# ScalarE before VectorE at the bank of transposed queries, and one ring of three PSUM banks in place of two and one

## The chip, the core and the metric

The kernel runs on one core of a Trainium2 chip. Five engines with queues of their own work side by side: TensorE (matmuls and transposes, written to PSUM as banks of 128 rows x 512 fp32), VectorE (DVE), ScalarE (ACT), GpSimd (POOL) and SyncE (SP, which issues most DMAs). They meet at semaphores. The metric is the device time of one execution in microseconds.

## What is computed

Causal attention with a gated memory part (4 batches, 8 heads, 576 rows, head size 64), and behind it a mixture of four experts with fixed weights per row, all in fp32:

```python
scores = scale * q @ k.T                       # causal, softmax -> a
local = a @ v
q_p = where(q > 0, q, exp(q) - 1) + 1
mem_out = (q_p @ M_prev) / (q_p @ z_prev + 1e-6)
x = g * mem_out + (1 - g) * local              # g = sigmoid(beta)
for e in range(4):
    out += p[:, e] * (relu(x @ w1[e]) @ w2[e])  # x: 2304 x 512, w1: 512 x 1024
```

## The kernel before

The expert part runs on TensorE with operands split in a high and a low fp32r half, three products for each. Its work comes in phases (one expert and half of its hidden columns for the row groups then open); mm1 makes the hidden tile h, ScalarE writes hh (L885) and VectorE hl (L886), mm2 makes y, and VectorE adds it to acc (L923). w_prep (L212) splits the weights: a cast on ScalarE (L225) or GpSimd (L227), then the difference on GpSimd (L228). The last eight of 24 phases handle the remaining rows in another form and hold no attention.

Attention of two heads of one batch is a task. The first run is written out by hand (first_run); 28 more tasks are cut into steps, and steps and parts of expert phases are issued alternately by a planner (the loop at the end), so that TensorE has matmuls of the expert part between the small pieces of attention. The first 12 tasks (query chunks 0 and 1, up to 188 us) are of the joint kind, the last 16 (chunks 2 to 4; their t_trq between 195 and 602 us) of the second kind. The order on every engine is the order of issue.

A task transposes queries (t_trq, tile tq), keys (t_trk, tk) and phi(q) (t_trqp, tp); s_qk makes scores (sp), VectorE masks them, ScalarE takes the exponential and scales; s_pt transposes the probabilities (tile pt, L353), evicted by ScalarE to pth (L660) and by VectorE to ptl (L662); s_o makes the output tile o, evicted by otmp (L573) and xr (L584). GpSimd scales phi(q) in place (qp, L345).

PSUM's eight banks: two for scores (tag qk), three for the expert part (moe), two in a ring for tq, tk, tp, o and the small transposes of the fifth chunk (tag to, function to_tile), and one for pt. A new tile of a ring waits for the last reader of the tile that had its bank. Two engines that read the same bank are also put one after the other, in the order of issue.

In t_trq of the second kind the bank tq is read by twelve instructions: split_q (ScalarE qa, qb; VectorE qa, qb, the low halves), split_k for 64 key columns (ScalarE kha, khb; VectorE kl twice), then four ScalarE copies to qz (L403). As issued, each group waits for the one before it.

Of the kernel before, what the change touches and what calls it, by code (L numbers as in the profile page):

```python
# [8 lines left out]
F32 = mybir.dt.float32  # L9
# [4 lines left out]
PSUM = bass.MemoryType.PSUM  # L14
# [35 lines left out]
def tile_attention_moe(  # L50
# [14 lines left out]
    P = 128  # L65
    B, H, S, D = q.shape
    NT, DM = out.shape
    E, _, F = w1.shape
# [5 lines left out]
    SCALE = -1.0 / (D ** 0.5)  # L74
# [34 lines left out]
    sp = ctx.enter_context(tc.tile_pool(name="sp", bufs=2))  # L109
    ps = ctx.enter_context(tc.tile_pool(name="ps", bufs=1, space=PSUM))  # L110
    own = ExitStack()
    att = own.enter_context(tc.tile_pool(name="att", bufs=2))

    def ctile(shape, dt, name, pool=cst):
# [23 lines left out]
    for i in range(2):  # L138
        o, d = i * 13 * P, {}
# [213 lines left out]
        nc.tensor.transpose(dst, src, ident[0:n, 0:n])  # L353

    def to_tile(name):
        return ps.tile([P, 512], F32, tag="to", name=name, bufs=2)

    A, Bh = slice(0, D), slice(D, P)

    def split_q(pt, qa, qb, n, scale):  # L360
        nc.scalar.activation(qa[A, 0:n], pt[A, 0:n], AF.Copy, scale=scale)
        nc.scalar.activation(qb[Bh, 0:n], pt[Bh, 0:n], AF.Copy, scale=scale)
        nc.vector.scalar_tensor_tensor(
            qa[Bh, 0:n], pt[A, 0:n], scale, f(qa[A, 0:n]), ALU.mult, ALU.subtract
        )
        nc.vector.scalar_tensor_tensor(
            qb[A, 0:n], pt[Bh, 0:n], scale, f(qb[Bh, 0:n]), ALU.mult, ALU.subtract
        )

    def split_k(pt, qk, c0, n, joint=False):  # L370
        o = slice(c0, c0 + n)
        for x, k_ in ((A, qk["kha"]), (Bh, qk["khb"])):
            nc.scalar.activation(k_[x, o], pt[x, 0:n], AF.Copy)
        for h, (x, k_) in enumerate(((A, qk["kha"]), (Bh, qk["khb"]))):
            l_ = qk["qz"][x, h * GW : h * GW + n] if joint else qk["kl"][x, o]
            nc.vector.tensor_tensor(l_, pt[x, 0:n], f(k_[x, o]), ALU.subtract)
# [12 lines left out]
    def t_trq(t):  # L389
        pt = to_tile(f"tq{t.i}")  # L390
        qk, last = t.qk, t.nk == NCH
        w = len(t.cs) * P
        for i in range(len(t.cs)):

            tr(pt[:, i * P : (i + 1) * P], flat(t.nat["q"][:, i]), P)
        if last:
            tr(pt[:, w : w + P], flat(t.nat["k"][:, 4]), P)
        split_q(pt, qk["qa"], qk["qb"], w, SCALE)
        if last:
            split_k(pt[:, w:], qk, 4 * P, D)  # L400
            for h, x in enumerate((A, Bh)):
                for o, a, b_ in ((h * GW, 0, GW), (2 * GW + h * D, w - D, w)):
                    nc.scalar.activation(  # L403
                        qk["qz"][x, o : o + b_ - a], pt[x, a:b_], AF.Copy, scale=SCALE
                    )

    def t_cpq(t):
        dup_k(t.qk, 4 * P, D, copier(t))

    def t_trk(t):  # L410
        pt = to_tile(f"tk{t.i}")
        m = min(t.nk, NCH - 1)
        for c in range(m):
            tr(pt[:, c * P : (c + 1) * P], flat(t.nat["k"][:, c]), P)
        split_k(pt, t.qk, 0, m * P, t.joint)
        if t.joint:
            t_cpk(t)

# [107 lines left out]
    def j_pt(i):  # L526
        s = slots[i]
        c, t = s.c, s.t
        qc = slice(c * P, (c + 1) * P)
        pt = ps.tile([P, 512], F32, tag="pt", name=f"pt{i}", bufs=1)  # L530
        pt = pt[:, 0 : 2 * (c + 1) * P].rearrange("p (h j q) -> p h j q", h=2, q=P)
        for hd in range(2):
            for j in range(c + 1):
                tr(pt[:, hd, j], s.s3[:, hd, j * P : (j + 1) * P], P)
        s.p4 = {
            x: PT[t.i % 2][x].rearrange("p j q -> p (j q)")[:, 0 : 4 * GW].rearrange(
                "p (h j q) -> p h j q", h=2, q=GW
            )
            for x in "hl"
        }  # L540
        dh, dl = (s.p4[x][:, :, 0 : c + 1, qc] for x in "hl")
        if c == 0:
            pt, dh, dl = pt[:, :, 0], dh[:, :, 0], dl[:, :, 0]
        nc.scalar.activation(dh, pt, AF.Copy)
        nc.vector.tensor_tensor(dl, pt, f(dh), ALU.subtract)
# [118 lines left out]
    def s_pt(i, last=False):  # L664
        s = slots[i]
        c, t = s.c, s.t
        qo = c * P - t.q0
        if last:
            pt = to_tile(f"pt{i}_4")

            m = rows(4)
            tr(pt[0:m, 0:P], s.s[:, 4 * P : S], P)
            src = pt[0:m, 0:P].rearrange("p (h q) -> p h q", h=2)
            hi = [PT[h]["h"][:, 4, qo : qo + D] for h in range(2)]
            evict([(src[:, h], hi[h][0:m], hi[h][m:P]) for h in range(2)])
            return
        pt = ps.tile([P, 512], F32, tag="pt", name=f"pt{i}", bufs=1)
        n = min(c + 1, 4)
        for j in range(n):
            tr(pt[:, j * P : (j + 1) * P], s.s[:, j * P : (j + 1) * P], P)  # L680
        if c < 4:
            src = pt[:, 0 : n * P].rearrange("p (j q) -> p j q", q=P)
            evict([(src, *(PT[s.hd][x][:, 0:n, qo : qo + P] for x in "hl"))])
        else:
            src = pt.rearrange("p (j h q) -> p h j q", j=4, h=2)
            evict(
                [(src[:, h], *(PT[h][x][:, 0:n, qo : qo + D] for x in "hl")) for h in range(2)]
            )
# [95 lines left out]
    for i, s in slots.items():  # L784
        w = wid(s.c)
# [184 lines left out]

    def open_last():
        own.close()
        pool = fin["pool"] = ctx.enter_context(tc.tile_pool(name="fin", bufs=1))

        def new(shape, dt, name):
            return pool.tile(shape, dt, tag=name, name=name, bufs=1)

        fin["x"] = {
            n: [new([P, 2, DM], F32R, f"{n}{z}") for z in "hl"]
            for n in ("b11", "t1", "t2", "b21", "t3", "t4", "b22")  # L980
        }
        fin["w"] = [
            new([P, 2, 7, GW], F32R, "wu"),
            w1all[:, 0 : 14 * GW].rearrange("p (z n f) -> p z n f", z=2, n=7),
        ]
        fin["s"] = [new([P, 4, GW], F32, f"sw{j}") for j in range(1)]

    def x_steps():
        x = fin["x"]
        t_ = {}  # L990

        def raw(k, c):
            return xr[:, 2 * (k // 2) + c, DM * (k % 2) : DM * (k % 2) + DM]

        def hi(n, c, src):
            nc.scalar.activation(x[n][0][:, c], src(), AF.Copy)

        def lo(n, c, src, eng):
            eng.tensor_tensor(x[n][1][:, c], src(), f(x[n][0][:, c]), ALU.subtract)

        def diff(n, c, tag, a, b_):
            t_[n, c] = ps.tile([P, 512], F32, tag=tag, name=f"{n}_{c}", bufs=2)
            nc.vector.tensor_tensor(t_[n, c], a(), b_(), ALU.subtract)

        V, G = nc.vector, nc.gpsimd
        out_ = []

        def both(fn, *args):
            out_.extend(lambda c=c: fn(c, *args) for c in range(2))

        def get(k, c):
            return t_[k, c] if isinstance(k, str) else raw(k, c)

        def D_(c, n, tag, a, b_):
            diff(n, c, tag, lambda: get(a, c), lambda: get(b_, c))

        def H_(c, n, k):
            hi(n, c, lambda: get(k, c))

        def L_(c, n, k, eng):  # L1020
            lo(n, c, lambda: get(k, c), eng)

        both(H_, "b11", 0)
        both(D_, "t1", "qk", 1, 0)
        both(L_, "b11", 0, V)
        both(H_, "t1", "t1")
        both(D_, "t2", "to", 3, "t1")
        both(L_, "t1", "t1", V)
        both(H_, "t2", "t2")
        both(D_, "t4", "qk", 2, "t2")  # L1030
        both(L_, "t2", "t2", V)
        both(H_, "t4", "t4")
        both(D_, "t3", "to", 3, 1)
        both(L_, "t4", "t4", V)
        both(H_, "t3", "t3")
        both(L_, "t3", "t3", V)
        late = len(out_)
        both(H_, "b21", 2)
        both(L_, "b21", 2, G)
        both(H_, "b22", 3)  # L1040
        both(L_, "b22", 3, G)
        return out_[:late], out_[late:]
# [43 lines left out]
    def pass_parts(i):  # L1086
# [5 lines left out]
        def prod(pr, key, wn, xn, new):  # L1092
            def run():
                if new:
                    tag, nb = {"x": ("to", 2), "z": ("qk", 2), "y": ("pt", 1)}[key]
                    bank[pr, key] = ps.tile(
                        [P, 512], F32, tag=tag, name=f"{key}{i}_{pr}", bufs=nb
                    )
                k_, n = bank[pr, key], 0
# [130 lines left out]
    def first_run():  # L1230
# [110 lines left out]
        def f_pt(i):  # L1341
# [2 lines left out]
            ptp[i] = (  # L1344
                moe_bank(f"ptf{i}")
                if c
                else ps.tile([P, 512], F32, tag="pt", name=f"ptf{i}", bufs=1)
            )
            pt4 = ptp[i][:, 0 : 2 * (c + 1) * P].rearrange("p (h j q) -> p h j q", h=2, q=P)
            for hd in range(2):  # L1350
# [167 lines left out]
    with tc.manual_schedule():  # L1518
# [7 lines left out]
        for i in range(2):  # L1526
            nc.gpsimd.memset(f(QK[i]["qz"]), 0.0)
            nc.gpsimd.memset(f(QK[i]["qa"][:, 3 * P :]), 0.0)
        first_run()
        phases = [phase_parts(i) for i in range(PASS)]  # L1530
        pcost = [sum(c for c, _ in ph) for ph in phases]

# [88 lines left out]
```

## Time and profile before

| | us |
|---|---|
| median of three runs | 1000.37 (999.36 to 1000.77) |
| profiled execution | 1000.42 |
| its span | 998.6 |
| TensorE busy | 983.3 |
| VectorE / ScalarE / GpSimd busy | 650.7 / 565.9 / 593.3 |

TensorE is the engine that is never long idle. Its ends are modelled in the profile, so that the distance from one start to the next is the surer measure of a lost time. VectorE, ScalarE and GpSimd are idle a third of the span or more; their idle time matters only where TensorE waits for what they do next.

### The profile page before, as it was taken

The numbers are of one execution on the slowest core, as the hardware profiler recorded it, in microseconds if no ns is written. First come the engines' busy times: TensorE is split into PE (matmuls) and PEld (weight loads), VectorE is DVE, ScalarE is ACT, GpSimd is POOL, SyncE is SP. The second block draws the span as 40 slices with busy tenths as digits, with TensorE's granted clock in tenths as the row PEclk, the third lists the DMA queues.
The fourth block names the chain that finished last, engine by engine and source line by source line (L and its number), as shares of the span: only waits on it lengthen the run. The fifth ranks groups of instructions, "written<-read, shape, count | busy, mean of one in ns | idle before, by whom it ended". The sixth has DMA issues, their size and how long they took to land.

```text
span 998.6 us, 16042 instructions
## 1 busy us (share of the span) xinstructions
PE 983.3 (98%) x5118; PEld 824.7 (83%) x5118; DVE 650.7 (65%) x1668; ACT 565.9 (57%) x1350; POOL 593.3 (59%) x601
## 2 busy tenths in 40 slices
PE   8999999999999999999999999999999999999998
PEld 6889878877888888888888888888888888888887
DVE  6888887878877777777788787755244252442533
ACT  7687866666666677766666666554334243242430
POOL 6898856755754667756574655386363563635620
PEclk9999999999999999999999999999999999999999
DMA  6676544544443345554444433131121121111102
GB/s 166 177 196 170 142 129 122 151 118 118 127 112 100 94 139 161 149 138 115 109 126 118 106 90 87 43 127 55 51 64 43 48 59 53 54 42 53 53 1 85
DMA packets 185268, 102.16 MB, mean 102 GB/s; under 512 B 96224, under 2 KB 163552, under 8 KB 185184
## 3 DMA queue, kind: packets, MB, share of 16 engines
q1 hardware_dynamic: 184880, 101.00, 37.1%
q8 instruction: 41, 0.67, 0.3%
q14 instruction: 43, 0.35, 0.1%
q10 hardware_dynamic: 304, 0.14, 0.1%
HBM read 90.09 MB, written 4.72 MB: 95 GB/s over the span
## 4 chain that ended last, share of the span: by engine, by line
PE 82%; DVE 6%; ACT 4%; POOL 3%; issue 3%; DMA 2%; SPq 0%; POOLq 0%; ACTq 0%; DVEq 0%
PE h L876 18%; PE y L1184 17%; PE y L907 16%; PE x L1106 9%; PE z L1106 4%; PE pt L353 3%; PE o L721 3%; PE sp L611 3%; PE y L1106 2%; POOL w2l L228 1%; POOL w L228 1%; DMA stg<-in_moe_w_dram 1%; PE sp L473 1%; PE o L559 1%; DVE acc L923 1%
## 5 line engine op out<-in xcount | busy, mean ns | idle before, releaser
L228 POOL TENSOR_TENSOR w2l<-stg,w2h 128x512 fp32r<-128x512 f32 x128 | 168.0, 1316 | 152.4 <-ACT w2h L225 147.7
L876 PE MATMUL h<-xh,w 128*128 128x512 f32 (+1 forms) x768 | 246.8, 371 | 0.0
L228 POOL TENSOR_TENSOR w<-stg,w 128x512 fp32r<-128x512 f32 x96 | 127.1, 1329 | 153.5 <-ACT w L225 133.7
L876 PEld LDWEIGHTS h<-xh,w 128*128 128x128 f32 x768 | 139.3, 190 | 17.7 <-POOL w L228 0.4
L876 PE MATMUL h<-xl,w 128*128 128x512 f32 (+1 forms) x384 | 137.0, 357 | 0.0
L907 PE MATMUL y<-w2h,hh 128*128 128x512 f32 x320 | 135.8, 424 | 0.5 <-DVE hl L886 0.5
L907 PE MATMUL y<-w2l,hh 128*128 128x512 f32 x320 | 125.8, 393 | 1.0 <-POOL w2l L228 1.0
L907 PE MATMUL y<-w2h,hl 128*128 128x512 f32 x320 | 126.3, 395 | 0.0
L1201 DVE SCALAR_TENSOR_TENSOR acc<-y,pn,acc 128x512 f32<-128x512 f32 (+1 forms) x57 | 41.6, 740 | 82.2 <-PE y L1184 82.2
L876 PEld LDWEIGHTS h<-xl,w 128*128 128x128 f32 x384 | 73.2, 191 | 5.8
L660 ACT ACTIVATE pth<-pt 128x384 fp32r<-128x384 f32 (+3 forms) x128 | 49.6, 419 | 47.6 <-PE pt L353 46.7
L907 PEld LDWEIGHTS y<-w2h,hl 128*128 128x128 f32 x320 | 60.0, 188 | 14.3 <-DVE hl L886 0.8
L907 PEld LDWEIGHTS y<-w2l,hh 128*128 128x128 f32 x320 | 60.6, 189 | 10.1 <-POOL w2l L228 2.9
L885 ACT ACTIVATE hh<-h 128x512 fp32r<-128x512 f32 (+1 forms) x96 | 50.5, 526 | 32.5 <-PE h L876 31.2
L907 PEld LDWEIGHTS y<-w2h,hh 128*128 128x128 f32 x320 | 60.4, 189 | 8.6 <-DVE hl L886 0.7
L886 DVE SCALAR_TENSOR_TENSOR hl<-h,hh 128x512 fp32r<-128x512 f32 (+1 forms) x96 | 57.4, 598 | 14.0 <-ACT hh L885 12.7
L353 PE MATMUL pt<-ident,s 128*128 128x128 f32 (+1 forms) x376 | 61.2, 273 | 2.1 <-DVE ptl L662 1.0
L353 PEld LDWEIGHTS pt<-ident,s 128*128 128x128 f32 (+1 forms) x376 | 46.7, 139 | 17.5 <-PE y L907 1.8
L1130 DVE TENSOR_TENSOR cp_a<-y,cp_a 128x512 f32<-128x512 f32 x16 | 11.1, 692 | 71.4 <-PE y L1106 71.4
L225 ACT ACTIVATE w<-stg 128x512 fp32r<-128x512 f32 x92 | 57.1, 626 | 0.7
L923 DVE SCALAR_TENSOR_TENSOR acc<-y,pn,acc 128x512 f32<-128x512 f32 x70 | 52.0, 743 | 6.0 <-PE y L907 5.5
L635 ACT ACTIVATE s<-s,st 128x384 f32<-128x384 f32 (+2 forms) x80 | 54.7, 684 | 1.0 <-DVE st L619 0.7
(274 smaller groups left out, 2571.9 us busy)
## 6 DMA issues: line engine op xcount, KB each, us to landing
stg<-in_moe_w_dram SPq DMA_DIRECT2D x256, 256.0 KB, 2.9
natall<-in_k_dram SPq DMA_DIRECT2D x34, 128.0 KB, 2.6
natall<-in_v_dram SPq DMA_DIRECT2D x32, 128.0 KB, 3.1
natall<-in_q_dram SPq DMA_DIRECT2D x60, 64.0 KB, 2.7
out_dram<-acc SPq DMA_DIRECT2D x15, 256.0 KB, 2.0
kha<-kha SPq DMA_DIRECT2D x16, 128.0 KB, 2.2
khb<-khb SPq DMA_DIRECT2D x16, 128.0 KB, 2.3
natall<-in_k_dram SPq DMA_DIRECT2D x28, 64.0 KB, 2.4
```

Source lines behind the costliest of these rows:

```text
L225: nc.scalar.activation(hi, t, AF.Copy)
L228: nc.gpsimd.tensor_tensor(lo, t, f(hi), ALU.subtract)
L353: nc.tensor.transpose(dst, src, ident[0:n, 0:n])
L635: nc.scalar.activation(s.s[:, 0:w], s.s[:, 0:w], AF.Exp, bias=s.st[:, 0:1], scale=-1.0, accum_out=s.st[:, 2:3],)
L660: nc.scalar.activation(dh, src, AF.Copy)
L876: nc.tensor.matmul(pt[0][:, cols], lhsT=w_[:, c], rhs=x_[:, c, cols], start=(c == 0 and z == 0), stop=(c == NKD - 1 and z == 2),)
L885: nc.scalar.activation(h_, pt[0][:, cols], AF.Relu)
L886: nc.vector.scalar_tensor_tensor(l_, pt[0][:, cols], 0.0, f(h_), ALU.max, ALU.subtract)
L907: nc.tensor.matmul(pt[0], lhsT=h_[fc][:, tk], rhs=w_, start=(fc == 0 and z == 0), stop=(fc == HF - 1 and z == 2),)
L923: nc.vector.scalar_tensor_tensor(acc[g, tt], pt[0], pe, acc[g, tt], ALU.mult, ALU.add)
L1106: nc.tensor.matmul(k_, lhsT=w_[:, c], rhs=x_[:, c], start=new and n == 0, stop=n == 5, skip_group_check=True,)
L1184: nc.tensor.matmul(y0, lhsT=a[:, tk], rhs=w_[:, x0:x1], start=(fc == 0 and z == 0), stop=(fc == HF - 1 and z == 2),)
```

## The change

split_q and split_k are each cut in two functions, one with the ScalarE copies (q_hi, k_hi) and one with VectorE's differences (q_lo, k_lo). t_trq of the second kind calls q_hi, k_hi and the four qz copies first, then q_lo and k_lo. Other callers keep their order.

The banks of the tags to and pt move out of the pool ps into pools that open_banks opens: psf (two and one, for the first run), psa (three banks with the tag to, from the end of the first run to the end of attention; pt comes from to_tile then), and psx (two and one, for the last phases).

```diff
+    def open_banks(name):
+        if "own" in banks:
+            banks["own"].close()
+        banks["own"] = ctx if name == "psx" else ExitStack()
+        banks["pool"] = banks["own"].enter_context(tc.tile_pool(name=name, bufs=1, space=PSUM))
+        banks["to"] = 3 if name == "psa" else 2
...
     def to_tile(name):
-        return ps.tile([P, 512], F32, tag="to", name=name, bufs=2)
+        return banks["pool"].tile([P, 512], F32, tag="to", name=name, bufs=banks["to"])
...
-        split_q(pt, qk["qa"], qk["qb"], w, SCALE)
+        q_hi(pt, qk["qa"], qk["qb"], w, SCALE)
         if last:
-            split_k(pt[:, w:], qk, 4 * P, D)
+            k_hi(pt[:, w:], qk, 4 * P, D)
             for h, x in enumerate((A, Bh)):
                 for o, a, b_ in ((h * GW, 0, GW), (2 * GW + h * D, w - D, w)):
                     nc.scalar.activation(
                         qk["qz"][x, o : o + b_ - a], pt[x, a:b_], AF.Copy, scale=SCALE
                     )
+        q_lo(pt, qk["qa"], qk["qb"], w, SCALE)
+        if last:
+            k_lo(pt[:, w:], qk, 4 * P, D)
...
-        pt = ps.tile([P, 512], F32, tag="pt", name=f"pt{i}", bufs=1)
+        pt = to_tile(f"pt{i}")
...
         first_run()
+        open_banks("psa")
```

On each engine the instructions stand in the same order as before; what differs is what they wait for. ScalarE at t_trq of the task that the profile shows at 301 us (tq16), before; a name in brackets is the engine whose semaphore is waited for, a line without brackets waits for nothing:

```order
L361 ACTIVATE qa0_78<-tq16_4046 64x384 [waits PE_49]
L362 ACTIVATE qb0_79<-tq16_4046 64x384
L373 ACTIVATE kha0_83<-tq16_4046 64x64 [waits DVE_49]
L373 ACTIVATE khb0_84<-tq16_4046 64x64
L403 ACTIVATE qz0_80<-tq16_4046 64x256 [waits DVE_49]
L403 ACTIVATE qz0_80<-tq16_4046 64x64
```

The same place after:

```order
L375 ACTIVATE qa0_81<-tq16_4053 64x384 [waits PE_49]
L376 ACTIVATE qb0_82<-tq16_4053 64x384
L389 ACTIVATE kha0_86<-tq16_4053 64x64
L389 ACTIVATE khb0_87<-tq16_4053 64x64
L422 ACTIVATE qz0_83<-tq16_4053 64x256
L422 ACTIVATE qz0_83<-tq16_4053 64x64
```

The two waits for VectorE are gone; VectorE's first instruction on the bank now waits for ScalarE's last copy in place of its second, and VectorE's third no longer waits.

TensorE at the first t_trq of the second kind (tp11 and pt44 are the next two tiles that take a bank; tq12 was emptied before them), before:

```order
L353 MATMUL tp11_2915<-ident_67,qp11_2575 128x128 [waits PE_49,DVE_49,Activation_49,Pool_49]
L353 MATMUL tp11_2915<-ident_67,qp11_2575 128x128
L876 MATMUL h8_0_2889<-xh_99,w1_109 128x512
...
L876 MATMUL h8_1_2927<-xh_99,w1_109 128x512 [waits Pool_49]
L353 MATMUL pt44_2937<-ident_67,s44_2797 128x128 x2
```

And after:

```order
L363 MATMUL tp11_2922<-ident_70,qp11_2582 128x128 [waits PE_49,Pool_49]
L363 MATMUL tp11_2922<-ident_70,qp11_2582 128x128
L899 MATMUL h8_0_2896<-xh_102,w1_112 128x512
...
L899 MATMUL h8_1_2934<-xh_102,w1_112 128x512 [waits Pool_49]
L363 MATMUL pt44_2944<-ident_70,s44_2804 128x128 [waits DVE_49,PE_49,Activation_49]
```

The wait for the readers of tq12 has moved from tp11 to pt44.

## Rows read from the trace of the kernel before

**Rows 1.** The page: span, busy time (share) of the engines, TensorE's granted clock in 40 slices.

```profile
span 998.6 us, 16042 instructions
...
PE 983.3 (98%) x5118; PEld 824.7 (83%) x5118; DVE 650.7 (65%) x1668; ACT 565.9 (57%) x1350; POOL 593.3 (59%) x601
...
PEclk9999999999999999999999999999999999999999
```

**Rows 2.** Who waited for whom: engine, line, releaser: us in total, times, longest.

```profile
ACT kha L373 <- DVE qb L366: 23.9, 16, 3.0
...
ACT qz L403 <- DVE kl L376: 8.4, 16, 0.5
```

**Rows 3.** ScalarE's timeline, 300 to 306: start, length, what [idle before <- releaser].

```profile
302.96 0.22 ACT L373 ACTIVATE kha<-tq 64x64 fp32r<-64x64 f32 x1 [1.19 <-DVE qb L366]
...
303.94 0.99 ACT L403 ACTIVATE qz<-tq 64x256 fp32r<-64x256 f32 x4 [0.52 <-DVE kl L376]
304.96 0.60 ACT L885 ACTIVATE hh<-h 128x512 fp32r<-128x512 f32 x1
```

**Rows 4.** VectorE's timeline in the same task.

```profile
301.80 0.55 DVE L363 SCALAR_TENSOR_TENSOR qa<-tq,qa 64x384 fp32r<-64x384 f32 x1 [0.85 <-ACT qb L362]
...
303.45 0.22 DVE L376 TENSOR_TENSOR kl<-tq,kha 64x64 fp32r<-64x64 f32 x1 [0.53 <-ACT khb L373]
...
305.58 0.69 DVE L886 SCALAR_TENSOR_TENSOR hl<-h,hh 128x512 fp32r<-128x512 f32 x1 [1.68 <-ACT hh L885]
```

**Rows 5.** TensorE's timeline at the first task of the second kind.

```profile
199.37 0.40 PE L876 MATMUL h<-xh,w 128*128 128x512 f32 x1
201.61 0.41 PE L353 MATMUL tp<-ident,qp 128*128 128x128 f32 x2 [1.84 <-ACT qz L403]
```

**Rows 6.** The stretch behind it: length, TensorE busy (instructions), granted clock, DMA share, GB/s.

```profile
203.00:206.40 3.40, 3.40 (x10) 0.50 0.69 174
```

**Rows 7.** TensorE's timeline at two tiles of probabilities, pt71 and pt126.

```profile
340.37 0.39 PE L876 MATMUL h<-xh,w 128*128 128x512 f32 x1
341.19 0.52 PE L353 MATMUL pt<-ident,s 128*128 128x128 f32 x3 [0.42 <-ACT ex L308]
...
633.14 0.40 PE L907 MATMUL y<-w2h,hl 128*128 128x512 f32 x1
633.66 0.52 PE L353 MATMUL pt<-ident,s 128*128 128x128 f32 x3
```

**Rows 8.** ScalarE, GpSimd and TensorE in the task at 414 us.

```profile
415.13 0.22 ACT L373 ACTIVATE kha<-tq 64x64 fp32r<-64x64 f32 x1 [2.38 <-DVE qb L366]
...
419.65 1.30 POOL L228 TENSOR_TENSOR w<-stg,w 128x512 fp32r<-128x512 f32 x1 [0.52 <-ACT w L225]
420.90 0.83 POOL L345 TENSOR_TENSOR qp<-qp,rn 128x384 f32<-128x384 f32 x1
...
421.79 0.55 PE L353 MATMUL tp<-ident,qp 128*128 128x128 f32 x3 [1.60 <-POOL qp L345]
```

**Rows 9.** TensorE's timeline behind the task at 383.6 us.

```profile
389.14 0.50 PE L907 MATMUL y<-w2h,hh 128*128 128x512 f32 x1 [0.52 <-DVE hl L886]
...
392.61 0.50 PE L907 MATMUL y<-w2l,hh 128*128 128x512 f32 x1 [1.03 <-POOL w2l L228]
```

**Rows 10.** VectorE and TensorE at the end of the first run.

```profile
30.81 0.44 PE L353 MATMUL tq<-ident,natall 128*128 128x128 f32 x2
...
31.52 0.43 DVE L376 TENSOR_TENSOR qz<-tk,khb 64x256 fp32r<-64x256 f32 x1
...
36.52 0.30 PE L473 MATMUL sp<-khb,qb 128*128 128x128 f32 x1 [0.98 <-DMA khb<-khb]
```

**Rows 11.** VectorE and TensorE at pt50.

```profile
229.00 0.76 DVE L662 TENSOR_TENSOR ptl<-pt,pth 128x256 fp32r<-128x256 f32 x2 [0.27 <-ACT pth L660]
...
229.90 0.63 PE L353 MATMUL pt<-ident,s 128*128 128x128 f32 x4 [0.96 <-DVE ptl L662]
```

**Rows 12.** Stretch: length, busy PE, PEld, DVE, ACT, POOL (instructions), clock, DMA.

```profile
201.00:231.00 30.00, 28.43 (x142) 23.44 (x143) 23.06 (x64) 19.84 (x53) 15.65 (x16) 0.94 0.45 120
```

More of the change, by code (lines that the diff above doesn't have):

```diff
@@ L111, in tile_attention_moe @@
     own = ExitStack()
+    banks = {}
+    def open_banks(name):
[4 more added lines that the diff above has]
+        banks["to"] = 3 if name == "psa" else 2
+    open_banks("psf")
     att = own.enter_context(tc.tile_pool(name="att", bufs=2))
@@ L355, in to_tile, with q_hi, q_lo @@
     def to_tile(name):
-        return ps.tile([P, 512], F32, tag="to", name=name, bufs=2)
+        return banks["pool"].tile([P, 512], F32, tag="to", name=name, bufs=banks["to"])
     A, Bh = slice(0, D), slice(D, P)
     def split_q(pt, qa, qb, n, scale):
+        q_hi(pt, qa, qb, n, scale)
+        q_lo(pt, qa, qb, n, scale)
+    def q_hi(pt, qa, qb, n, scale):
         nc.scalar.activation(qa[A, 0:n], pt[A, 0:n], AF.Copy, scale=scale)
         nc.scalar.activation(qb[Bh, 0:n], pt[Bh, 0:n], AF.Copy, scale=scale)
+    def q_lo(pt, qa, qb, n, scale):
         nc.vector.scalar_tensor_tensor(
@@ L368, in split_q, with k_hi @@
         )
-    def split_k(pt, qk, c0, n, joint=False):
+    def k_hi(pt, qk, c0, n):
         o = slice(c0, c0 + n)
@@ L373, in split_k, with k_lo @@
             nc.scalar.activation(k_[x, o], pt[x, 0:n], AF.Copy)
+    def k_lo(pt, qk, c0, n, joint=False):
+        o = slice(c0, c0 + n)
         for h, (x, k_) in enumerate(((A, qk["kha"]), (Bh, qk["khb"]))):
@@ L414, in t_trk @@
             tr(pt[:, c * P : (c + 1) * P], flat(t.nat["k"][:, c]), P)
-        split_k(pt, t.qk, 0, m * P, t.joint)
+        k_hi(pt, t.qk, 0, m * P)
+        k_lo(pt, t.qk, 0, m * P, t.joint)
         if t.joint:
@@ L676, in s_pt @@
             return
-        pt = ps.tile([P, 512], F32, tag="pt", name=f"pt{i}", bufs=1)
+        pt = to_tile(f"pt{i}")
         n = min(c + 1, 4)
@@ L972, in open_last @@
         own.close()
+        open_banks("psx")
         pool = fin["pool"] = ctx.enter_context(tc.tile_pool(name="fin", bufs=1))
@@ L1001, in diff @@
         def diff(n, c, tag, a, b_):
-            t_[n, c] = ps.tile([P, 512], F32, tag=tag, name=f"{n}_{c}", bufs=2)
+            pool = ps if tag == "qk" else banks["pool"]
+            t_[n, c] = pool.tile([P, 512], F32, tag=tag, name=f"{n}_{c}", bufs=2)
             nc.vector.tensor_tensor(t_[n, c], a(), b_(), ALU.subtract)
@@ L1095, in run @@
                     tag, nb = {"x": ("to", 2), "z": ("qk", 2), "y": ("pt", 1)}[key]
-                    bank[pr, key] = ps.tile(
+                    pool = ps if tag == "qk" else banks["pool"]
+                    bank[pr, key] = pool.tile(
                         [P, 512], F32, tag=tag, name=f"{key}{i}_{pr}", bufs=nb
@@ L1346, in f_pt @@
                 if c
-                else ps.tile([P, 512], F32, tag="pt", name=f"ptf{i}", bufs=1)
+                else banks["pool"].tile([P, 512], F32, tag="pt", name=f"ptf{i}", bufs=1)
             )
```

## Prediction, made before the changed kernel ran

> **What bounds the kernel now.** I read the page first. TensorE is busy 983.3 of 998.6 us and its clock is at the full level almost everywhere [rows 1]. So the time is TensorE's work plus the places where TensorE stands still, and an edit that moves no TensorE instruction can win only at those places. That caps it: 15.3 us of idle span, part of it the start-up, plus what the clock lost. The second view is who waits for whom. ScalarE stands 23.9 us in 16 waits before kha for VectorE's qb, and 8.4 us in 16 waits before qz for VectorE's kl [rows 2]. That is once per task of the second kind (16 tasks, first at 198 us, last at 602 us), always while t_trq empties its bank of transposes. One such task in the steady part shows the pattern: ScalarE idles 1.19 us before kha, 0.52 us before qz, and only then reaches the hidden layer's hh at 304.96 [rows 3]. VectorE idles 0.85, 0.53 and 1.68 us [rows 4]. Neither is TensorE's path by itself. So I looked through TensorE's timeline for starts that come later than the usual start-to-start distance (0.23 us for 512 columns, 0.12 us for 256), and asked for each which reader of which bank it waited for. The reader is to see in the rows below that most of these places are either a bank that was not free, or work queued behind ScalarE's pause.
>
> **The change part by part.** The order of instructions on all five engines is the same before and after; only waits differ. I go through the places where TensorE stands.
>
> *The first bank of transposed queries, 201.6 us.* TensorE's matmul at 199.37 is followed by tp at 201.61 with ScalarE's qz as releaser [rows 5]: 2.24 us start to start in place of 0.23, so 2.0 lost. Before, tp takes the bank of tq two allocations back in the ring of two; after, with three banks in turn, it takes the bank of pt42, whose last reader was done six us earlier. The 2.0 go. Next is the wait of the following pt, which now takes tq's bank: its last reader (kl) ended at 200.49 in the trace and pt began at 203.46, so even 2.0 us earlier it finds the bank free. [...] Sum 3.7.
>
> *The bank of probabilities.* pt71 starts 0.82 us after the matmul before it (0.59 late), pt126 0.52 us (0.29 late) [rows 7]. The profile names ScalarE work for the one and nobody for the other, but VectorE's ptl of the pt before ended 0.15 us ahead of each start, which is the gap every such release shows. Three more are of this kind: pt51 at 233.74 (0.24), pt76 at 368.66 (0.57), pt86 at 426.60 (0.18). After, these five take a bank whose readers were done 3.6 us or more before. Next late is ScalarE's scaled row s, 1.2 us or more ahead in each case but pt86 and pt126 (0.6 and 0.4), so all 1.9 us go.
>
> *Work queued behind ScalarE's pause.* In the task at 414 us ScalarE idles 2.38 us before kha (and 0.53 before qz, as in [rows 3]). Behind it stand two weight casts, GpSimd's subtraction at 419.65 waits for the second, GpSimd's qp stands behind that, and TensorE waits 1.60 us for qp at 421.79 [rows 8]. With no pause ScalarE is 2.9 us ahead, qp ends near 418.8 instead of 421.73, and TensorE would reach it at 420.1. So 1.6 to 1.8 go; I take 1.7. In the task at 383.6 us ScalarE gains the usual 1.19 + 0.52 = 1.7. TensorE stands there for hl (start to start 0.80 in place of 0.12, so 0.68) and then for w2l (1.42 in place of 0.23, so 1.19) [rows 9]. Both hang on ScalarE's queue behind qz. hl ended 0.06 us before its user, so 1.7 us earlier frees it entirely; w2l ends 1.7 earlier while TensorE arrives 1.87 earlier, so 0.1 stays. I take 1.8.
>
> *What gets later.* VectorE now waits for all eight ScalarE copies, not two. In the task of [rows 4] ScalarE's eight end at 301.77 + 0.46 + 0.99 = 303.2, and VectorE's four (1.12 + 0.46) end at 304.8 instead of 303.91: 0.9 later. This holds in 13 of 16 tasks. What stands behind on VectorE is hl at 305.58, which waits for ScalarE's hh, and hh is 1.7 earlier; so VectorE is free before it is asked. In two tasks (441.4, 575.2) an accumulation behind kl starts 0.9 later; nobody waits for it within the next 2 us. I cost this at nothing; without that cover it is 0.9 per task. The bank itself comes free at 304.8 instead of 304.9.
>
> *A new wait at the start.* The pool of three banks is opened after the first run, and its first tile, tq0, gets the bank that tk0 has just filled. tq0 started at 30.81; tk0's last reader, VectorE's second kl, ended at 31.95 [rows 10]. With 0.1 for the release tq0 starts 1.24 later. But TensorE stands 0.98 us at 36.52 for the landing of khb, a transfer that ScalarE issues at 31.3 ahead of anything tq0 feeds [rows 10]. So 0.98 of the 1.24 is paid there anyway. Bounds 0 to 1.24; I take 0.3.
>
> *What doesn't come through.* pt50 at 229.90 stands 0.96 us for ptl, whose row ends at 229.76 [rows 11]. Three back in the new ring is the same bank, so this wait stays in the program; it shrinks only as far as VectorE runs earlier. When TensorE is 3.7 us ahead at 206, VectorE and ScalarE must catch up. VectorE is busy 23.06 of the 30 us from 201 to 231 [rows 12], so it can make up some 7 us in that stretch if it isn't waiting for TensorE. Two places have less than 1 us of slack there (hl at 219, pt50). I take off 0.6 in all; bounds: nothing (pt50's 0.96 gained besides), and 3.7 (the whole lead handed back).
>
> Sum: 3.7 + 1.9 + 1.7 + 1.8 - 0.3 - 0.6 = 8.2 us. The profiled execution took 1000.42 (span 998.6 and 1.8 around it), the median of the three runs is 1000.37, so both give **992.2 us**. After 665 us TensorE stands nowhere over 0.1 us, so what is won before stays won.
>
> **The rivals.**
> *VectorE is next.* The 3.7 us lead at 206 is handed back by 231 because VectorE and GpSimd, not the bank, set the pace there. For it: VectorE was itself 1.7 us behind the copies at 222, and the rows at 229.9 show TensorE on VectorE. Against: 7 us of idle VectorE in those 30. It leaves 8.2 - 3.1 = 5.1: 995.3 us.
> *The clock at the start.* The new pause at 30.8 follows six us in which TensorE had several gaps; if it drops the clock as at 203, that costs 1.7 more and the full 1.24: 1000.4 - (8.2 - 2.6) = 994.8 us. Against: the wait of 0.98 at 36.5 and of 1.60 at 421.8 left the clock at the full level. [...]
> *It does nothing.* The bank's emptying is as long as before (the same twelve instructions one after another), so another data wait takes each place: within 0.2% of 1000.4. Against: four of the six places lose their wait in the program.
> *Slower: one bank in turn.* With one ring TensorE must take the bank three back even if another is free. If VectorE, now last at every bank, is the late one at all 16 tasks, each costs its 0.9 us: 14.4 us, against the 8.2 won, some 1006 us. It decides where VectorE is some 2 us later than in the trace: outside the tasks at 224 and 414, where ScalarE's copies end 3 us earlier, the smallest distance from the last reader of a query bank to that bank's next user is 1.9 us. [...]
>
> **How the numbers follow.** Forecast 0.62 (its own range 989.5 to 994.5), VectorE next 0.16, clock at the start 0.08, nothing 0.08, slower 0.06. Range 989.0 to 996.5: from all terms at their upper bound (pt50 gained, nothing taken off) and the spread of the runs, up to the second and third case. 0.2% is about what a measurement of this kernel can tell from no change. Faster by more: 0.62 + 0.16 + 0.08 = 0.86; same 0.08; slower 0.06.
>
> **What would show it.** Right: no pause at tp11 and the clock at the full level through 200 to 210; ScalarE's eight copies without a gap, 1.7 us shorter; no pause at tp20 and at the five pt; TensorE's second slice of 25 us the same length within 0.5 us although tq0 waits until VectorE's kl. Wrong: pauses at hl near 216 or at pt49 and pt50 of 1 us and more (VectorE next), a clock at the low level near 32 us, or TensorE waiting for a kl or ptl of the bank three back in task after task.

## The result, and the profile after

The changed kernel takes 991.31 us (median of four executions, 991.04 to 992.45; before beside it 1000.57, 999.36 to 1000.77). The ratio is 0.9914, interval 0.9899 to 0.993: faster by under 1%, some 8.6 us by the ratio and 9.3 between the two medians, and inside the range. The forecast time, 992.2, was 0.9 us too long. As shown below, two terms in the sum were wrong and nearly cancelled.

Page of the changed kernel: span, busy time of the engines, TensorE's granted clock [rows 1].

```profile
span 990.7 us, 16062 instructions
...
PE 981.3 (99%) x5118; PEld 825.2 (83%) x5118; DVE 647.9 (65%) x1668; ACT 566.9 (57%) x1350; POOL 591.1 (60%) x601
...
PEclk9999999999999999999999999999999999999999
```

TensorE's busy time fell by 2.0 us, its idle span from 15.3 to 9.4; the busy times of VectorE, ScalarE and GpSimd differ from before by 1.0 to 2.8 us. ScalarE's two groups of 16 waits [rows 2] are no longer in the list of waits. In their place VectorE waits for ScalarE (engine, line, releaser: us in total, times, longest):

```profile
DVE qa L379 <- ACT qz L422: 26.8, 14, 2.5
```

The task of [rows 3, 4], ScalarE and then VectorE (timeline: start, length, what, idle before and its releaser):

```profile
298.24 0.49 ACT L376 ACTIVATE qb<-tq 64x384 fp32r<-64x384 f32 x1
298.74 0.22 ACT L389 ACTIVATE kha<-tq 64x64 fp32r<-64x64 f32 x1
298.98 0.22 ACT L389 ACTIVATE khb<-tq 64x64 fp32r<-64x64 f32 x1
299.22 0.99 ACT L422 ACTIVATE qz<-tq 64x256 fp32r<-64x256 f32 x4
300.23 0.60 ACT L908 ACTIVATE hh<-h 128x512 fp32r<-128x512 f32 x1
```

```profile
300.24 0.55 DVE L379 SCALAR_TENSOR_TENSOR qa<-tq,qa 64x384 fp32r<-64x384 f32 x1 [2.45 <-ACT qz L422]
...
301.87 0.69 DVE L909 SCALAR_TENSOR_TENSOR hl<-h,hh 128x512 fp32r<-128x512 f32 x1
```

ScalarE runs through, and hh starts right behind qz. VectorE waits once, 2.45 us; behind kl it goes straight into hl, without the 1.68 us of [rows 4]. TensorE at tp11 [rows 5] and the clock behind it [rows 6] (stretch: length, busy PE, PEld, DVE, ACT, POOL, granted clock, DMA):

```profile
200.51 0.39 PE L899 MATMUL h<-xh,w 128*128 128x512 f32 x1
200.74 0.38 PE L363 MATMUL tp<-ident,qp 128*128 128x128 f32 x2
```

```profile
202.00:205.40 3.40, 3.40 (x19) 2.78 (x18) 3.29 (x11) 2.73 (x9) 3.32 (x4) 1.00 0.61 166
```

Start to start 0.23 us in place of 2.24, and the granted clock is 1.00 in place of 0.50. At tp20 [rows 8] GpSimd's qp is now done 1.2 us before its user:

```profile
412.52 0.83 POOL L355 TENSOR_TENSOR qp<-qp,rn 128x384 f32<-128x384 f32 x1
```

```profile
414.30 0.39 PE L899 MATMUL h<-xh,w 128*128 128x512 f32 x1
414.54 0.49 PE L363 MATMUL tp<-ident,qp 128*128 128x128 f32 x3
```

One place got worse. At 217 TensorE waits for ScalarE's hh, and hh stands behind a scaled row for which ScalarE waited 2.96 us on VectorE:

```profile
214.90 0.62 ACT L679 ACTIVATE s<-s,st 128x384 f32<-128x384 f32 x1 [2.96 <-DVE st L672]
...
216.30 0.60 ACT L908 ACTIVATE hh<-h 128x512 fp32r<-128x512 f32 x1
```

```profile
216.12 0.39 PE L930 MATMUL y<-w2h,hl 128*128 128x512 f32 x1
217.04 0.47 PE L930 MATMUL y<-w2h,hh 128*128 128x512 f32 x1 [0.54 <-ACT hh L908]
```

The order of TensorE's instructions is the same in all kernels here, so start times can be compared one matmul at a time. I do that in one table behind the experiments.

### The profile page after: what moved, and what is told of

Same layout as the page of the kernel before. It is cut to its first block, busy times and chain, and to the rows that moved or that the text cites. A ratio compares the mean times of both kernels' runs of the same rounds, so it can differ in the third digit from the quotient of the medians.

```text
span 990.7 us, 16062 instructions
## 1 busy us (share of the span) xinstructions
PE 981.3 (99%) x5118; PEld 825.2 (83%) x5118; DVE 647.9 (65%) x1668; ACT 566.9 (57%) x1350; POOL 591.1 (60%) x601
## 4 chain that ended last, share of the span: by engine, by line
PE 90%; DVE 2%; POOL 2%; ACT 2%; DMA 2%; issue 1%; SPq 0%; POOLq 0%; DVEq 0%; ACTq 0%
PE y L930 21%; PE h L899 20%; PE y L1210 18%; PE x L1132 9%; PE z L1132 4%; PE pt L363 4%; PE sp L634 3%; PE o L744 3%; PE y L1132 2%; DMA stg<-in_moe_w_dram 1%; PE tq L363 1%; PE sp L496 1%; PE o L582 1%; PE tk L363 1%; PE tp L363 1%
## 5 line engine op out<-in xcount | busy, mean ns | idle before, releaser
L908 ACT ACTIVATE hh<-h 128x512 fp32r<-128x512 f32 (+1 forms) x96 | 50.4, 525 | 35.6 <-PE h L899 33.6
L685 DVE TENSOR_TENSOR ptl<-pt,pth 128x384 fp32r<-128x384 f32 (+1 forms) x96 | 51.5, 550 | 8.2 <-ACT pth L683 5.6
```

Source lines behind the costliest of these rows:

```text
L685: nc.vector.tensor_tensor(dl, src, f(dh), ALU.subtract)
L908: nc.scalar.activation(h_, pt[0][:, cols], AF.Relu)
```

## The experiments

**The kernel before, once more.** In the profile after, TensorE's first 12 us take 1.4 us longer than in the profile before, at code that the change doesn't touch. So the kernel before was traced a second time, without an edit.

> The kernel before once more, for its trace. The three profiles with both parts of the change show the first 12 us 1.4 us longer than the profiles of before, of the order alone and of the ring alone (TensorE's first rows run at half pace until 9.6 us, not 5.0). Theory (this differs from execution to execution): the first 12 us may come out long here too, and the five executions of before, or those with the change, don't all agree. Rival (the change sets it): the first 12 us of before are as in its first profile, tq0 starts at 30.8.

Measured: 1000.58 us. Eight matmuls of the start-up (tile pf) in the first profile of before, and in this one:

```profile
5.79 0.93 PE L1281 MATMUL pf<-tw,tw 64*128 64x128 f32 x8 [0.61 <-DVE tw L1270]
```

```profile
5.84 1.65 PE L1281 MATMUL pf<-tw,tw 64*128 64x128 f32 x8 [0.61 <-DVE tw L1270]
```

So the long start comes with the kernel before too, and the change isn't needed for it. (TensorE runs at half pace there: behind pf, the two transposes of tg start 0.21 us apart, in the first trace 0.11.) Of the ten traces of this study seven have the long start: all six with both parts of the change, and of the other four only this one. This trace, and those of one fill, two fills and the early pool below, also come from another chip than the other experiments. That the start differs from execution to execution of one kernel on one chip is thus likely, since three of the changed kernel's four executions are 0.9 to 1.4 us shorter than its profiled one, but it isn't shown. The second trace showed more than was asked. TensorE stands at tp11 as in [rows 5], 2.24 us from start to start, and this time the clock does not fall as it did in [rows 6]:

```profile
202.57 0.41 PE L353 MATMUL tp<-ident,qp 128*128 128x128 f32 x2 [1.84 <-ACT qz L403]
```

```profile
203.00:206.40 3.40, 3.40 (x19) 2.75 (x19) 3.00 (x9) 3.03 (x10) 3.23 (x4) 1.00 0.76 197
```

The same pause, once with the fall and once without. The two executions end within 0.2 us of each other only because the first had the short start. Of the 17 executions of before that ran beside the order alone, the ring alone and the unused tile (below), 3 have a mean granted clock of 0.998, as has the profile with the fall; 2 have 0.999 and 12 have 1.000. So most executions of before probably have no fall.

**A pause made on purpose.** To see whether a pause of TensorE in dense work brings the clock down, VectorE fills tp24's bank with zeros n times ahead of the transposes:

```diff
+        if t.i == 24:
+            for _ in range(n):
+                nc.vector.memset(pt, 0.0)
```

> The changed kernel with extra work that changes no result: VectorE fills tp24's bank four times with zeros ahead of TensorE's transposes into it (near 513 us), so that TensorE stands still once, in dense work, for about 2 us or a little more. Theory (the pause at tp11 took the clock down): behind the pause the granted clock falls to 0.50 for some 3.4 us, so the time from the pause on is later than in the changed kernel by the pause plus 1.7 us. Rival (the fall at 203 us has another cause): the clock stays at 1.00 and the work behind it is later by the pause alone.

> The changed kernel with one fill of tp24's bank by VectorE ahead of TensorE's transposes (extra work that changes no result). Four fills made a pause of 3.4 us, each further one 0.67, so one should make 1.4 us. Theory (a pause takes the clock down only from about 2 us on: 1.76 and 1.62 left it up, 2.0 did not): the clock stays at 1.00 and the work behind is later by 1.4 us. Rival (any pause of over 1 us amid dense work takes it down): 1.4 + 1.6 us later.

> The same with two fills: a pause of 2.1 us, as long as the 2.0 us at tp11 in the kernel before. Theory: the clock falls to 0.50 for some 3.4 us right behind the pause, the work behind is later by 2.1 + 1.6 = 3.7 us. Rival (the fall at 203 us needed something else besides the pause): 2.1 us later and the clock stays at 1.00.

TensorE's timeline at tp24, and a stretch behind it (busy times and granted clock, columns as above), one fill:

```profile
522.04 0.39 PE L902 MATMUL h<-xh,w 128*128 128x512 f32 x1
523.71 0.52 PE L363 MATMUL tp<-ident,qp 128*128 128x128 f32 x3 [1.28 <-DVE tp L449]
```

```profile
523.90:527.30 3.40, 3.40 (x20) 2.93 (x19) 2.09 (x4) 3.00 (x7) 0.46 (x1) 1.00 0.00 0
```

Two fills:

```profile
522.45 0.39 PE L902 MATMUL h<-xh,w 128*128 128x512 f32 x1
524.78 0.52 PE L363 MATMUL tp<-ident,qp 128*128 128x128 f32 x3 [1.95 <-DVE tp L449]
...
525.37 0.39 PE L902 MATMUL h<-xl,w 128*128 128x512 f32 x1
525.60 0.39 PE L902 MATMUL h<-xh,w 128*128 128x512 f32 x1
```

```profile
525.90:529.30 3.40, 3.40 (x12) 2.81 (x11) 2.27 (x4) 3.38 (x8) 1.30 (x2) 0.51 0.00 0
```

Four fills:

```profile
522.12 0.39 PE L902 MATMUL h<-xh,w 128*128 128x512 f32 x1
525.78 0.52 PE L363 MATMUL tp<-ident,qp 128*128 128x128 f32 x3 [3.27 <-DVE tp L449]
```

```profile
526.20:529.60 3.40, 3.40 (x12) 2.72 (x12) 2.20 (x4) 2.63 (x6) 0.00 (x0) 0.50 0.00 0
```

Measured, one execution each: 994.46, 997.09 and 998.06 us, against 992.45 for the changed kernel's profiled execution; 0.5 to 0.9 us of each difference was lost ahead of the pause. Beyond the usual 0.22 us the pauses are 1.44, 2.11 and 3.44 us (for four fills about 2 was expected). Behind the first the matmuls keep pace; behind the others they lose 1.58 and 1.62 us more by 532 us, and from then on to the end the loss stays. In all three the clock and the loss behind the pause came out as the theory said. A pause of 2.1 us can thus bring the low level (0.51 over 3.4 us), at 1.58 us, and the pause at tp11 is enough to explain the fall of [rows 6]. It isn't certain to bring it: the 2.0 us of tp11 did in one of two traces, and 1.44, 1.76 (tp20) and 1.35 us (tq0 after) did not in any (1.00 over the 3.4 us behind each: 523.9 to 527.3 with one fill, 421.8 to 425.2 in the first trace of before, 33.6 to 37.0 in the changed kernel). So the theory's "only from about 2 us on" fits these traces, but each length was tried once or a few times, and it is no shown limit. What makes the two tp11 differ is not shown: no run here tests it.

**The new order alone** (two banks and one, as before).

```diff
-        split_q(pt, qk["qa"], qk["qb"], w, SCALE)
+        q_hi(pt, qk["qa"], qk["qb"], w, SCALE)
         if last:
-            split_k(pt[:, w:], qk, 4 * P, D)
+            k_hi(pt[:, w:], qk, 4 * P, D)
...
+        q_lo(pt, qk["qa"], qk["qb"], w, SCALE)
+        if last:
+            k_lo(pt[:, w:], qk, 4 * P, D)
```

> The kernel before with the new order of t_trq alone (ScalarE's eight copies, then VectorE's four); the banks stay a ring of two and one bank for pt. Theory (the emptying order alone carries the places queued behind ScalarE's pause, the ring carries tp11 and the five pt): tp11 still takes tq12's bank, but VectorE's kl now ends near 200.0, so its pause shrinks from 1.84 to about 0.5 us and no fall of the clock follows: 1.4 + 1.7 gained; tp20 1.7 and y14 1.5 gained; the stalls of the five pt stay (1.9 not gained). In all 6 to 7 us less than before, about 994 us. Rival (the ring carries it, the order is a detail): tp11 and the clock fall stay, only tp20 and y14 go: 3.2 us, above 997 us.

Measured: 992.09 us (990.7 to 993.6), ratio 0.9923 (0.9909 to 0.9937). The theory's 994 was too long, the rival's 997 far off. At tp11 the pause is 0.50 us (0.73 less the usual 0.23), as expected:

```profile
199.12 0.40 PE L889 MATMUL h<-xh,w 128*128 128x512 f32 x1
199.85 0.41 PE L353 MATMUL tp<-ident,qp 128*128 128x128 f32 x2 [0.33 <-DVE kl L385]
```

What I had wrong is the pt: pt71 stands no more, although it still takes the single bank.

```profile
335.90 0.40 PE L889 MATMUL h<-xh,w 128*128 128x512 f32 x1
336.13 0.49 PE L353 MATMUL pt<-ident,s 128*128 128x128 f32 x3
```

VectorE tells why. The first rows are of before, where VectorE stands idle for ScalarE's otmp, which is queued behind ScalarE's pauses at the bank tq; the last is of the new order alone:

```profile
330.47 0.99 ACT L403 ACTIVATE qz<-tq 64x256 fp32r<-64x256 f32 x4 [0.52 <-DVE kl L376]
...
332.33 0.43 ACT L573 ACTIVATE otmp<-o 64x320 f32<-64x320 f32 x1
```

```profile
332.79 0.57 DVE L584 TENSOR_TENSOR xr<-o,otmp 64x256 f32<-64x256 f32 x2 [2.35 <-ACT otmp L573]
```

```profile
326.80 0.56 DVE L597 TENSOR_TENSOR xr<-o,otmp 64x256 f32<-64x256 f32 x2
```

VectorE is 6.0 us earlier there, TensorE ahead of pt71 only 4.47 (340.37 [rows 7] to 335.90), so ptl is done in time. Of the five pt only pt126 still waits for its bank. So 1.65 of the 1.9 that the theory left out was won, and pt50's 1.12 besides.

**The ring alone** (the changed kernel with t_trq as before).

```diff
-        q_hi(pt, qk["qa"], qk["qb"], w, SCALE)
+        split_q(pt, qk["qa"], qk["qb"], w, SCALE)
         if last:
             k_hi(pt[:, w:], qk, 4 * P, D)
+            k_lo(pt[:, w:], qk, 4 * P, D)
...
-        q_lo(pt, qk["qa"], qk["qb"], w, SCALE)
-        if last:
-            k_lo(pt[:, w:], qk, 4 * P, D)
```

> The changed kernel's ring of three with t_trq in the old order (ScalarE two, VectorE two, ScalarE two, VectorE two, ScalarE four). Theory: tp11's pause and the clock fall behind it go, a lead of some 3.5 us at 206, but ScalarE still needs 1.7 us more for each bank, so that much of this lead is handed back between 205 and 231 (at the scores of slot 46, at hl near 217, at pt50); the five pt gain 1.9 in part; tp20 (1.6 us) and y14 (1.5 us) stay as before. In all some 3 to 4 us less than before, about 997 us. Rival (the ring alone is enough, a bank is always free in time): 5.5 us and more, under 995 us. If the two parts only add, this run and the new order alone together give the 9.2 us of the change.

Measured: 997.99 us (997.81 to 1001.05), ratio 0.9986 (0.9977 to 0.9995): some 1.4 us less than before by the ratio, 2.3 between the medians. The theory's places are right, its 3 to 4 us were too much: the clock's 1.7 was in it, which only some executions have to win. ScalarE's waits are as in [rows 2], tp11 has no pause, and then the lead is handed back, at pt46 to VectorE and at 217 us to hh; pt50 and tp20 stand as in [rows 11] and [rows 8].

```profile
ACT kha L389 <- DVE qb L382: 23.9, 16, 3.1
```

```profile
206.81 0.87 PE L363 MATMUL pt<-ident,s 128*128 128x128 f32 x4 [0.75 <-DVE s L537]
...
228.79 0.63 PE L363 MATMUL pt<-ident,s 128*128 128x128 f32 x4 [0.98 <-DVE ptl L683]
...
419.83 0.55 PE L363 MATMUL tp<-ident,qp 128*128 128x128 f32 x3 [1.58 <-POOL qp L355]
```

**The new wait at the start.** First, an unused tile ahead of tq0 moves it to another bank of the new pool:

```diff
+        if name == "psa":
+            to_tile("skip")
```

> The changed kernel with one tile taken from the new pool and not used before tq0, so that tq0 doesn't get the bank that tk0 has just filled. Theory (the new wait is paid at the landing of khb anyway): tq0's pause of 1.6 us goes, the pause at the scores behind it grows by as much, the same time as the changed kernel within 0.3 us (a ratio to before of 0.991). Rival (the wait costs its length): 1.2 to 1.6 us less than the changed kernel, 2.9 less if it also cost clock.

Measured: 992.47 us (991.05 to 993.41), ratio 0.9923 (0.9911 to 0.9935). The edit did not take the wait away, so it can't tell the two apart. In the changed kernel, and with the unused tile:

```profile
33.61 0.41 PE L363 MATMUL tq<-ident,natall 128*128 128x128 f32 x2 [1.46 <-DMA mr<-in_M_prev_dram]
```

```profile
33.64 0.41 PE L365 MATMUL tq<-ident,natall 128*128 128x128 f32 x2 [1.45 <-DMA mr<-in_M_prev_dram]
```

(The profile names a DMA; in the program tq0 now also waits for tk0's transposes, ScalarE and VectorE, and VectorE's last kl ended 0.21 us before.) So the bank that tq0 gets doesn't decide. A wait for the readers of the pool that was closed, for whichever tile of the new pool comes first, would fit. To see it, the second edit opens the pool ahead of tk0:

```diff
         def f_go(j):
+            if j == 4:
+                open_banks("psa")
...
         first_run()
-        open_banks("psa")
```

> The changed kernel with the pool of three opened ahead of tk0 in place of behind it, so that tk0 and tq0 are two banks of the same ring and tq0 waits for no reader of tk0. (The unused tile ahead of tq0 had left this wait as it was.) Theory (the wait is paid at the landing of khb anyway): tq0's pause shrinks from 1.62 to about 0.3 us, the pause at the scores behind it grows from 0 to about 1, and from 40 us on every start is within 0.2 us of the changed kernel's, the start-up's own difference left out. Rival: 1.3 us earlier from there to the end.

Measured: 994.49 us in one execution. tq0's pause is gone, but the wait has gone to tk0, and sp0 stands for kha:

```profile
32.78 0.44 PE L363 MATMUL tk<-ident,natall 128*128 128x128 f32 x2 [0.93 <-DVE xl L1454]
...
33.52 0.38 PE L363 MATMUL tq<-ident,natall 128*128 128x128 f32 x2
...
39.12 0.30 PE L496 MATMUL sp<-kha,qa 128*128 128x128 f32 x1 [1.42 <-DMA kha<-kha]
```

Neither side had this. It does help with the question, what a wait costs at this place. Just ahead of tk0 this execution was 0.53 us behind the changed kernel's, at tk0 1.53, and at sp0's third matmul 1.54 (39.37 against 37.83): a wait of 1.0 ahead of tk0 is paid in full, since the transfers of kha and khb start from tk0. The 1.35 us behind tk0 are mostly paid at the landing anyway: at sp0's third matmul the changed kernel is 0.15 us better off against the first trace of before and 0.18 worse off against the second. In the ring alone, which has the same wait, 0.16 and 0.48 are lost. (From a tk at 119 us on another 0.4 us is lost in the kernel with the early pool; that was not followed up.)

## Where each microsecond went

How much earlier a kernel's matmul starts, counted only from the place above to this one (us; minus is later). The first column of measured values goes from the first trace of before to the changed kernel; the other three are against the second trace of before, in which the clock stayed up.

| place | predicted | changed, first trace | changed, second trace | order alone | ring alone |
|---|---|---|---|---|---|
| tq0 and sp0, 30 to 38 | -0.3 | +0.15 | -0.18 | -0.13 | -0.48 |
| tp11 | 2.0 | 2.02 | 2.00 | 1.51 | 2.00 |
| to tp12 (clock) | 1.7 | 1.62 | 0.03 | -0.03 | -0.52 |
| tp12 to pt48, 206 to 220 | -0.6 with the next | -1.09 | -0.39 | 0.21 | -1.47 |
| pt50 | | 1.13 | 1.13 | 1.12 | 0.01 |
| pt51, 71, 76, 86, 126 | 1.9 | 2.01 | 2.04 | 1.76 | 1.93 |
| y13 (376) | 0 | -0.34 | -0.28 | -0.28 | -0.50 |
| y14 (389 to 393) | 1.8 | 1.65 | 1.66 | 1.66 | 0.01 |
| tp20 | 1.7 | 1.74 | 1.73 | 1.75 | -0.01 |
| elsewhere | 0 | 0.54 | 0.51 | 0.42 | 0.21 |
| sum | 8.2 | 9.43 | 8.25 | 7.99 | 1.18 |

The row of the five pt also takes in small differences on the way to each; at the five starts themselves the four columns have 1.97, 1.93, 1.65 and 1.91. In the ring alone the row to tp12 holds no clock (that trace's mean granted clock is 1.000, where the one fall of before makes it 0.998), but waits.

One entry worked out: ahead of tp11 the second trace of before stands at 200.33 and the changed kernel at 200.51; tp11 starts at 202.57 and 200.74. So it goes from 0.17 behind to 1.83 ahead: 2.00.

## Why the prediction held, point by point

**Right.** tp11's 2.0, tp20's 1.7 and the five pt's 1.9 came as sized (2.0, 1.73, 1.93). At y14 the 1.8 measured 1.66, and at y13 0.28 was lost that I hadn't counted: at both TensorE now comes early enough to wait for GpSimd's w2l. The new wait at tq0 is mostly absorbed by khb's landing, as argued from [rows 10]; its cost lies between -0.15 and 0.18 in the changed kernel (up to 0.48 in the ring alone), where I took 0.3. The reason given for that wait (tq0 gets tk0's bank) was wrong: moved to another bank it waits just as long, and with the pool opened earlier the wait goes to tk0. VectorE as last reader of the query bank cost nothing: in the changed kernel no stall of TensorE names such a kl.

**Wrong: the clock, 1.7.** Of the 3.7 that the sum takes for tp11, 2.0 are the gap and 1.7 my estimate for the clock: half of the 3.40 us at 0.50 [rows 6], counted as lost to the gap and won with it. No run shows a gain of 1.7 there: measured were 1.62 against the first trace of before and 0.03 against the second. A gap of this length can cause the fall, as the two fills showed (0.51 behind 2.11 us). But the fall is no fixed part of the kernel before: the second trace has the gap and not the fall (1.00). And where it occurs, less than its length is won, since by 220 us 0.7 us more is handed back than in the other trace (1.09 against 0.39). By the clocks of the 17 executions, what a typical one gains from this term is near nothing. I had one execution, took what it showed for a property of the kernel, and its time matched the median only because its start was a short one.

**Wrong: what doesn't come through, -0.6.** It measured +0.74: the 206 to 220 stretch gave back 0.39, but pt50 gained 1.13. The step was "Three back in the new ring is the same bank, so this wait stays in the program; it shrinks only as far as VectorE runs earlier"; I didn't work out how much earlier that is. The rows of before were there, ScalarE and VectorE ahead of [rows 11]:

```profile
224.95 0.22 ACT L373 ACTIVATE kha<-tq 64x64 fp32r<-64x64 f32 x1 [2.90 <-DVE qb L366]
```

```profile
225.44 0.22 DVE L376 TENSOR_TENSOR kl<-tq,kha 64x64 fp32r<-64x64 f32 x1 [0.53 <-ACT khb L373]
...
227.79 0.21 DVE L648 TENSOR_SCALAR st<-st,ebp 128x1 f32<-128x1 f32 x1 [0.63 <-ACT s L635]
```

With the 0.27 of [rows 11] VectorE waits 1.43 us here for ScalarE, and ScalarE is late because of one of the pauses, 2.90 us long in this task (225.93 for qz before, 221.15 after: 4.8 us earlier where TensorE is 1.4 earlier). All of the 1.43 goes, more than the wait at pt50. After, VectorE works through and ptl starts at

```profile
226.03 0.75 DVE L685 TENSOR_TENSOR ptl<-pt,pth 128x256 fp32r<-128x256 f32 x2
```

in time for pt50 at 227.39. So, against the trace in which the clock stayed up, 1.7 too much at the clock and 1.3 too little here: the sum came right by luck.

**Wrong in its attribution.** I credited the ring with tp11 and the five pt. The runs show that either part alone wins most of both: 1.5 of tp11's 2.0 and 1.65 of the pt's 1.93 come with the order, 2.0 and 1.91 with the ring. y14, tp20 and pt50, 4.5 us, come with the order alone, and without it the ring hands 2 us back between 203 and 220. Order alone (8.0) and ring alone (1.2) add up to 9.2 where the whole is 8.25: some 3.1 us (1.5 at tp11, 1.6 at the pt) are in both, and the order saves the ring most of its losses. Beside the order the ring is worth 0.3: it wins 0.5 at tp11 and 0.3 at pt126 and loses 0.6 between 206 and 220. The times can't tell the changed kernel from the order alone (0.9899 to 0.993 against 0.9909 to 0.9937).

**The rivals.** VectorE next: its place appeared at 217 us, for 0.4 us (1.1 against the first trace) and not 3.1. The clock at the start: tq0's pause of 1.35 us left it up in all six traces that have it (1.00 from 33.6 to 37.0 in the changed kernel; the mean granted clock is 1.000 in four of the six, and 0.998 with two and with four fills, as one fall gives it). One ring in turn: from 200 us on no pause of TensorE over 0.1 us in the changed kernel is one for a bank of the ring, and no trace with the ring of three shows a fall of the clock, but for the pauses made on purpose (mean granted clock 1.000 in the other five). That the change does nothing is excluded: the interval of the ratio ends at 0.993. No kernel here beat the changed one by more than its spread.

**Left open:** what decides, at a pause of about 2 us, whether the clock falls; what decides between the short and the long start; and how far these 1.4 us account for the 3 us by which executions of before differ (998.56 to 1001.74), since only two of them have a trace.

## What to carry to other kernels

When an engine pauses in the middle of a row of small copies, price the pause at everything queued behind it, on that engine and on those that wait for it: here 1.2 + 0.5 us on ScalarE in the usual task, 16 times, stood behind nine of TensorE's stalls, which shrank or went with the order alone, most of them at lines that never touch the bank tq. Before adding up two edits, ask of each stall whether the other edit removes it too. And before counting on something that stands in a trace once, such as a fall of the clock, take a second trace of the same kernel.

## What the runs showed of the hardware

One pause of TensorE of 2.1 us amid dense work brought the granted clock to 0.51 over 3.4 us (525.90 to 529.30), at 1.58 us on top of the pause; behind 3.44 us of pause it was 0.50 and the cost 1.62, no more; behind 1.44 it was 1.00 and nothing more was lost. With two fills the low level set in only some 1.1 us after work had resumed: the matmuls at 524.78 to 525.60 still run at full pace (0.23 us from 525.37 to 525.60; 0.42 from 527.00 to 527.42). With four fills it was there within 0.5 us (525.78, and 0.50 from 526.20 on). The same 2.0 us pause had a fall once (0.50 from 203.0 to 206.4) and once not (1.00). At the start, the same eight matmuls took 0.93 or 1.65 us in two executions of one kernel (perhaps on two chips).
